# Three transfers and a copy re-timed at the head of a two-layer transformer kernel: the fourth group of x, Wk of the third group, tile 3

## The chip, the cores and the metric

The kernel runs on one core of a Trainium2 chip. The metric is device time in microseconds (us) of one execution; four executions of the kernel before took 1230.28 to 1231.41, median 1230.93. A core has a matrix engine (PE, with its weight loads PEld), VectorE (DVE), ScalarE (ACT), GpSimd (POOL) and SyncE (SP). Here SP issues nearly all loads from memory and the transposing DMAs, and POOL issues the DMAs that move attention data within the core.

## The reference

Input x has 2048 tokens of 1024 features. Two layers follow one another, with the same weights in both; each is attention and then a feed-forward part, both on a layer norm and both added to x. Cut to what matters:

```python
def _A_ref(x, wqkv, wo):                   # 32 heads of 32, window of 8 tokens, 2 apart
    q, k, v = split(x @ wqkv)              # wqkv is 1024 x 3072
    idx = pos[:, None] - 2 * arange(8)     # this token and 7 before it; masked where negative
    attn = softmax(where(mask, q . k[idx] * 32 ** -0.5, -1e9))
    return (attn . v[idx]) @ wo
def _B_ref(x, w1, b1, w2, b2):
    return gelu(x @ w1 + b1) @ w2 + b2     # 1024 -> 3584 -> 1024

for _ in range(2):
    x = x + _A_ref(layernorm(x), wqkv, wo)
    x = x + _B_ref(layernorm(x), w1, b1, w2, b2)
```

Data are bf16; sums in PE's accumulators are f32.

## The kernel before, in words

The 2048 tokens are cut into NG = 4 groups of T = 512, each of four tiles of 128 tokens. A group in a layer is a step n = 0 to 7 (n = 0 to 3 are groups 0 to 3 in layer one). x stays on the core in 16 tiles `x[0]` to `x[15]`; `load_x(g)` issues the four loads (256 KB each) of group g, and `load_x(3)` is the fourth group, `x[12]` to `x[15]`.

A step has these parts, each a Python generator that yields after each chunk of PE work:

- `gen_qkv(n)`: queries, keys and values of the group, eight chunks each. A chunk is eight matmuls (k = 0 to 7) into one accumulator bank `acc`, which ACT casts into `qT`, `kT` or `vT`.
- `gen_wo(n)`: the attention output `oT` times wo. For each tile and half of the features, eight matmuls run over c = 0 to 7, and DVE adds the result to x.
- `gen_ffn1(n)` and `gen_ffn2(n)`: the feed-forward part.

Between them is the attention proper. DVE multiplies queries and keys (`new_prod`, `add_prods`), POOL's DMAs gather the products by head (`gather`, into `abc` in the first steps), DVE and ACT form the softmax (`logits`, `weights`, giving `a`), POOL's DMAs spread its weights over the partitions (`spread`: four DMAs `abc<-a` of 256 KB), and `av(n, c)` on DVE multiplies them with the values and writes `oT[:, c]`. A list of side calls in `stage` says after which chunk of PE work such a call is emitted.

The layer norm gives normalized tiles `xn`, and `xnT`, their transpose, is what PE reads. Mostly a transposing DMA from SP makes it. At the head, PE transposes tiles 2 and 3 of group 0 itself (`transpose_on_pe`), between the rows of the first queries (`queries_of_raw`), and ACT copies the accumulator bank into `xnT` (`copy_transposed`, in as many pieces as `parts` names).

Weights come in halves: `load_qkv(which)` issues two loads of 1 MB, h0 for k = 0 to 3 and h1 for k = 4 to 7, of Wq (0), Wk (1) or Wv (2). All weights share `wpool` with five buffers, taken in turn, so a load waits until PE has made its last use of the half loaded five places earlier. In program order the halves at the head are: Wq h0, h1, Wk h0, h1, Wv h0, h1 of group 0, the same six of group 1, the same six of group 2, and then the two halves of wo for `gen_wo(0)`.

Each engine's instructions run in the order in which they stand on it. The Tile framework sets that order from a simulation; where the kernel wants its own, `InOrder` records each instruction, chains them while `on` is true, and `hold()` puts all later ones behind the last. For SP this is on at the head and ends with step 0. What stands there on SP before the change, in order: transposes of group 1 and of tiles 0 and 1 of group 2, `load_x(3)`, Wq h0, h1 and Wk h0 of group 1, the transposes of tiles 2 and 3 of group 2 (`ln_end`; they read `xn` in buffers named `qT`), and Wk h1, Wv h0, Wv h1 of group 1, and then Wq of group 2.

Step 1 is built with `mix=NCH // 2`: four query chunks, then keys and queries in turn, then the remaining keys; its Wv is loaded before the ninth chunk (`i == NCH`). Step 2 has all its queries first. The order on PE at the head is step 0's q, k, v, step 1's q, k, v, then queries, keys and two value chunks of step 2, then `gen_wo(0)`, and then the rest of step 2's values. `between(0, 1)`, after chunk 11 of step 1, holds `logits(0)`, `weights(0)` and `spread(0)`; `av(0, c)` follows from chunk 12 on, and `load_b1` issues four small POOL DMAs in step 2. The statistics of group 3's layer norm (`ln_stats_ahead(3)`, on ACT) are the first reader of `x[12]` to `x[15]`.

Of the kernel before, what the change touches and what calls it, by code (L numbers as in the profile page):

```python
# [17 lines left out]
def kernel(  # L18
# [19 lines left out]
    _, S, D = A_x.shape  # L38
# [12 lines left out]
    KD = D // P  # L51
    KF = F // P
    NCH = D // P
    HP = P // H
# [7 lines left out]
    wqkv_v = A_wqkv.rearrange("(k p) f -> p k f", p=P)  # L62
# [15 lines left out]
    def acc_tile():  # L78
        return psum.tile([P, T], F32, name="acc", bufs=8)
# [23 lines left out]
    vec, act, pool, sp = InOrder(nc.vector), InOrder(nc.scalar), InOrder(nc.gpsimd), InOrder(nc.sync)  # L103
# [6 lines left out]
    def pe(inst):  # L110
        if last_pe[0] is not None:
            dep_order(inst, last_pe[0], "PE program order")
        last_pe[0] = inst
        return inst

    def mm(*args, **kwargs):
        return pe(nc.tensor.matmul(*args, **kwargs))  # L117
# [3 lines left out]
    def load_x(g, t0=0, t1=NTT, engine=None):  # L121
        for tt in range(t0, t1):
            t = g * NTT + tt
            (engine or sp).dma_start(x[t][:], x_in[t * P:(t + 1) * P, :])

    def load_qkv(which, between=None):
        tiles = []
        for h in range(2):
            wt = wpool.tile([P, KD // 2, D], BF16, name="wt")
            sp.dma_start(wt[:], wqkv_v[:, h * (KD // 2):(h + 1) * (KD // 2), which * D:(which + 1) * D])  # L130
            if h == 0 and between:
                between()
            tiles.append(wt)
        return tiles
# [88 lines left out]
    def transpose_on_pe(xn, out, bank, parts=(0, KD)):  # L223
        pst = bank[:].bitcast(BF16).rearrange("p (k t) -> p k t", t=P)
        for k in range(KD):
            pe(nc.tensor.transpose(pst[:, k, :], xn[:, k * P:(k + 1) * P], ident[:]))  # L226
        copy_transposed(out, bank, parts)

    def copy_transposed(out, bank, parts):
        pst = bank[:].bitcast(BF16).rearrange("p (k t) -> p k t", t=P)  # L230
        for k0, k1 in zip(parts[:-1], parts[1:]):
            act.copy(out[:, k0:k1, :], pst[:, k0:k1, :])
# [8 lines left out]
    first_early, first_late = [], []  # L241
# [67 lines left out]
    def queries_of_raw(wq, qT):  # L309
        raw, spread_stats, rest = st.pop("raw")  # L310
        first = {}

        def row(c, k):
            if k == 0:
                first[c] = acc_tile()
            mm(first[c][:, 0:NT + 2], lhsT=wq[k // (KD // 2)][:, k % (KD // 2), c::NCH], rhs=raw[:, k, :],
               start=(k == 0), stop=(k == KD - 1), skip_group_check=True)

        part = attp.tile([P, NCH, NT], F32, name="abc")

        def finish(c):
            vec.scalar_tensor_tensor(out=part[:, c, :], in0=less, scalar=first[c][:, NT:NT + 1], in1=first[c][:, 0:NT],
                                     op0=ALU.mult, op1=ALU.add)
            pool.tensor_tensor(out=qT[:, c, 0:NT], in0=part[:, c, :], in1=rstd, op=ALU.mult)

        for k in range(KD):
            for c in range(7):
                row(c, k)
                if (k, c) == (0, 6):
                    bank = acc_tile()  # L330
                if (k, c) == (2, 6):
                    less, rstd = spread_stats(bank)
                    rest()
                if (k, c) in ((5, 3), (7, 6)):
                    transpose_on_pe(*first_late.pop(0), bank)
        act.on = False
        act.hold()
        for c in range(7):
            finish(c)
        for k in range(KD):  # L340
            row(7, k)
        vec.on = False
        return lambda: finish(7)
# [13 lines left out]
    def qkv_chunk(wts, c, xnT, ps=None, k0=0, k1=KD, t0=0, t1=NTT):  # L357
        if ps is None:
            ps = acc_tile()
        for k in range(k0, k1):  # L360
            mm(ps[:, t0 * P:t1 * P], lhsT=wts[k // (KD // 2)][:, k % (KD // 2), c::NCH], rhs=xnT[:, t0:t1, k, :],
               start=(k == 0), stop=(k == KD - 1), skip_group_check=t1 - t0 < NTT)
        return ps
# [21 lines left out]
    def gen_qkv(n, defer=False, qk_pool=None, v_late=False, qk_next=None, v_first=False, mix=0):  # L385
        g = n % NG
        xnT = xa.pop(n)
        s = st[n]
        s["prods"] = []
        qk_pool = qk_pool or attp  # L390
        if v_first:
            wv = load_qkv(2)
        wq = wq_first if n == 0 else load_qkv(0)
        if n > 0 and not v_first:
            wk = load_qkv(1)

        def values():
            vT = attp.tile([P, NCH, HALO + T], BF16, name="vT", bufs=2)
            s["vT"] = vT
            act.on = n > 2  # L400
            if g == 0:
                pool.memset(vT[:, :, 0:HALO], 0.0)
            else:
                (act.copy if n > 1 else pool.tensor_copy)(vT[:, :, 0:HALO], st[n - 1]["vT"][:, :, T:T + HALO])
            act.on = False
            for c in range(NCH):
                ps = qkv_chunk(wv, c, xnT)
                act.copy(vT[:, c, HALO:], ps[:])
                yield

        if v_first:
            yield from values()
            wk = load_qkv(1)
        qT = qk_pool.tile([P, NCH, T], BF16, name="qT")
        if n == 0:
            last = queries_of_raw(wq, qT)
            for xn, out in first_early:
                sp.dma_start_transpose(out, xn.rearrange("s (k p) -> s k p", p=P))
            wk = load_qkv(1, lambda: load_x(1, 2, 3))
            load_x(1, 3, 4)  # L420
            load_x(2)
            early_tiles = ln_early((1, None), (2, qk_next))
            for tt in range(2):
                next(early_tiles)
                if tt == 0:
                    last()
            wv = load_qkv(2)
            for _ in early_tiles:
                pass
            vec.hold()  # L430
            load_x(3)
            sp.on = False
            sp.hold()
        kT = qk_pool.tile([P, NCH, HALO + T], BF16, name="kT")
        s["qT"], s["kT"] = qT, kT
        act.on = n > 2
        if g == 0:
            pool.memset(kT[:, :, 0:HALO], 0.0)
        else:
            (act.copy if n > 1 else pool.tensor_copy)(kT[:, :, 0:HALO], st[n - 1]["kT"][:, :, T:T + HALO] if n < 3 else khalo[:])  # L440
        act.on = False

        def query(c):
            t0 = 2 if n == 0 else 0
            ps = qkv_chunk(wq, c, xnT, t0=t0)
            act.copy(qT[:, c, t0 * P:], ps[:, t0 * P:])

        def key(c):
            ps = qkv_chunk(wk, c, xnT)
            act.copy(kT[:, c, HALO:], ps[:])  # L450
            if not defer:
                new_prod(n, c)

        ahead = mix or NCH
        turns = [(query, c) for c in range(ahead)]
        for c in range(NCH):
            turns.append((key, c))
            if ahead + c < NCH:
                turns.append((query, ahead + c))
        for i, (chunk, c) in enumerate(turns):  # L460
            if i == NCH and n > 0 and not v_late and not v_first:
                wv = load_qkv(2)
            chunk(c)
            yield
        if g + 1 < NG and n > 1:
            act.copy(khalo[:], kT[:, :, T:T + HALO])
        if not v_first:
            if v_late:
                wv = load_qkv(2)
            yield from values()  # L470
# [49 lines left out]
    def between(n, m):  # L520

        vec.on = True
        for c in range(2):
            new_prod(m, c, False)
        add_prods(m, 0)
        logits(n)
        add_prods(m, 1)
        weights(n)
        spread(n)
        new_prod(m, 2, False)  # L530
        add_prods(m)
        vec.on = False

    def spread(n):

        s = st[n]
        a = s.pop("a")
        abc = attp.tile([P, NTT, W, P], BF16, name="abc")
        s["abc"] = abc
        s["oT"] = attp.tile([P, NCH, T], BF16, name="qT" if n == N - 1 else "oT")  # L540
        for j in range(HP):
            pool.dma_start(abc[j::HP, :, :, :], a[:])

    def av(n, c):
        s = st[n]
# [183 lines left out]
    n = N - 2  # L729
# [35 lines left out]
```

## Time and profile before

| | us |
|---|---|
| median of four runs | 1230.93 (1230.28 to 1231.41) |
| profiled execution, whole | 1230.72 |
| its span | 1228.9 |
| PE busy | 1220.3 (99%) |
| DVE busy | 865.8 (70%) |
| ACT busy | 315.0 (26%) |
| POOL busy | 121.8 (10%) |
| TensorE clock granted | 1.0 throughout |
| DMA: 227.18 MB, mean | 185 GB/s |
| in the first 59 us | 304 GB/s, DMA share 1.03 |

A row of a timeline gives the start, the length, the engine and line, the operation, output<-input by the program's names, the number of instructions merged, and in brackets the idle time of the engine before it and what ended that. L92 and L117 are helpers through which nearly all instructions go, so one reads by tiles. SPq is SP's queue: its lengths are those of issues, and when the data land is told by the trace's landing records. Times are counted from the start of the span.

### The profile page before, as it was taken

What the parts mean: (1) busy time and instruction counts of PE and PEld (TensorE: products, weight loads), DVE (VectorE), ACT (ScalarE), POOL (GpSimd) and SP (SyncE); (2) the same over time, 40 slices, a digit from 0 to 9 for tenths busy, and PEclk for the clock granted to TensorE, in tenths of its full rate; (3) what the DMA queues carried; (4) which work ended last, traced back from release to release, by engine and by line L of the source; (5) the groups of instructions that cost most, each with busy time, mean ns of one, the idle gap of its engine ahead of it and who ended that gap; (6) DMA issues with size and microseconds to landing.
All of it is one profiled execution on the core that took longest, in us unless ns stands there. A gap on an engine that the chain in (4) does not pass through costs nothing.

```text
span 1228.9 us, 13973 instructions
## 1 busy us (share of the span) xinstructions
PE 1220.3 (99%) x5719; PEld 632.1 (51%) x5769; DVE 865.8 (70%) x926; ACT 315.0 (26%) x497; POOL 121.8 (10%) x217
## 2 busy tenths in 40 slices
PE   9999999999999999999999999999999999999998
PEld 7666544456444564446544465444654444444444
DVE  8989898998898999375993759937598797011001
ACT  5343253014410234202441024410244001300310
POOL 2430006010101101100001000000000002000000
PEclk9999999999999999999999999999999999999999
DMA  9974665766637645856547565576664558446441
GB/s 317 291 206 157 184 201 182 201 175 203 217 130 245 186 150 166 237 172 176 159 158 232 171 171 180 157 216 201 171 202 144 188 194 211 147 160 194 157 136 51
DMA packets 225824, 227.18 MB, mean 185 GB/s; under 512 B 74000, under 2 KB 192928, under 8 KB 223712
## 3 DMA queue, kind: packets, MB, share of 16 engines
q1 hardware_dynamic: 216304, 208.17, 55.5%
q0 software_dynamic: 8880, 17.07, 4.2%
q8 instruction: 45, 0.74, 0.2%
q10 hardware_dynamic: 576, 1.05, 0.2%
q14 instruction: 19, 0.16, 0.0%
HBM read 189.01 MB, written 4.19 MB: 157 GB/s over the span
## 4 chain that ended last, share of the span: by engine, by line
PE 98%; DMA 1%; DVE 0%; issue 0%; ACT 0%
PE acc L117 98%; DMA wt<-in_A_wqkv_dram 0%; DMA x<-in_A_x_dram 0%; DVE stats L92 0%; PE acc L226 0%; ACT xnT L92 0%; ACT vT L92 0%; PE acc L289 0%; DVE mvs L92 0%; DVE x L92 0%; ACT stds L92 0%
## 5 line engine op out<-in xcount | busy, mean ns | idle before, releaser
L117 PE MATMUL acc<-xnT,wt 128*128 128x512 bf16 (+1 forms) x3328 | 713.2, 377 | 1.5 <-DMA wt<-in_A_wqkv_dram 1.3
L117 PEld LDWEIGHTS <-wt 128*128 128x128 bf16 x3392 | 400.6, 119 | 320.7 <-DMA wt<-in_A_wqkv_dram 1.9
L117 PE MATMUL acc<-wt,hT 128*128 128x512 bf16 (+1 forms) x1780 | 386.0, 376 | 2.1
L117 PEld LDWEIGHTS <-hT 128*128 128x128 bf16 x1820 | 178.1, 98 | 209.0
L92 DVE TENSOR_TENSOR big<-big 128x2048 bf16<-128x2048 bf16 (+2 forms) x185 | 245.1, 1353 | 2.2
L92 ACT ACTIVATE hT<-acc,b1T 128x512 bf16<-128x512 f32 x224 | 151.8, 689 | 323.2 <-PE acc L117 323.1
L92 DVE TENSOR_TENSOR big<-qT,kT 128x4096 bf16<-128x4096 bf16 x64 | 143.9, 2285 | 37.5 <-ACT kT L92 35.8
L92 DVE TENSOR_TENSOR big<-abc,vT 128x4096 bf16<-128x4096 bf16 x64 | 144.7, 2285 | 14.2 <-DMA abc<-a 10.2
L92 DVE TENSOR_TENSOR tmp<-acc,b2bc 128x512 f32<-128x512 f32 x56 | 38.6, 690 | 153.7 <-PE acc L117 150.5
L92 ACT CAST qT<-acc 128x512 bf16<-128x512 f32 (+1 forms) x64 | 35.5, 559 | 276.6 <-PE acc L117 276.6
L117 PE MATMUL acc<-wt,oT 128*128 128x512 bf16 x440 | 97.4, 379 | 0.4
L92 DVE BATCH_NORM_STATS2 stats<-x 128x6 f32<-128x512 bf16 x116 | 77.5, 682 | 4.7 <-DMA x<-in_A_x_dram 3.6
L117 PEld LDWEIGHTS <-oT 128*128 128x128 bf16 x448 | 43.7, 98 | 52.9 <-DVE oT L92 0.4
L92 DVE TENSOR_TENSOR x<-acc,big 128x512 bf16<-128x512 f32 (+1 forms) x9 | 5.7, 633 | 90.0 <-PE acc L117 90.0
L92 POOL TENSOR_TENSOR rstd<-mv,eps_t 128x1 f32<-128x1 f32 x48 | 14.7, 306 | 502.0 <-DVE mv L92 502.0
L92 ACT CAST vT<-acc 128x512 bf16<-128x512 f32 x64 | 37.5, 586 | 101.8 <-PE acc L117 101.8
L92 ACT CAST kT<-acc 128x512 bf16<-128x512 f32 x64 | 37.2, 584 | 61.8 <-PE acc L117 61.7
L92 DVE TENSOR_TENSOR x<-acc,x 128x512 bf16<-128x512 f32 x64 | 42.9, 671 | 4.1 <-PE acc L117 3.7
L92 DVE TENSOR_SCALAR xn<-x,mv,rstd 128x1024 bf16<-128x1024 bf16 x48 | 26.2, 546 | 20.1 <-POOL rstd L92 19.9
L92 DVE TENSOR_TENSOR x<-tmp,x 128x512 bf16<-128x512 f32 x56 | 38.6, 690 | 1.4
L92 POOL DMA_DIRECT2D big<-big x24 | 13.3, 565 | 212.2 <-DVE big L92 212.2
L92 ACT ACT_TABLE_LOAD x17 | 21.8, 1283 | 43.6 <-DVE e L92 30.5
(82 smaller groups left out, 304.1 us busy)
## 6 DMA issues: line engine op xcount, KB each, us to landing
wt<-in_B_w_dram SPq DMA_DIRECT2D x56, 1024.0 KB, 5.6
wt<-in_B_w_dram SPq DMA_DIRECT2D x64, 896.0 KB, 4.9
wt<-in_A_wqkv_dram SPq DMA_DIRECT2D x46, 1024.0 KB, 5.6
wt<-in_A_wo_dram SPq DMA_DIRECT2D x16, 1024.0 KB, 5.0
abc<-a POOLq DMA_DIRECT2D x32, 256.0 KB, 5.2
big<-big POOLq DMA_DIRECT2D x24, 256.0 KB, 3.9
out_dram<-x SPq DMA_DIRECT2D x31, 128.0 KB, 1.8
x<-in_A_x_dram SPq DMA_DIRECT2D x14, 256.0 KB, 5.4
```

The costliest lines, as they stand in the source:

```text
L92: inst = f(*args, **kwargs)
L117: return pe(nc.tensor.matmul(*args, **kwargs))
```

## The change

Three edits:

1. `load_x(3)` is taken out of step 0, where it stood behind the early transposes, and is issued in step 1 behind the loads of its Wv (`n == 1`, before the ninth chunk). On SP the four loads now stand between Wv h1 of group 1 and Wq h0 of group 2.
2. `load_qkv` gets an argument `behind`: its first half waits on a semaphore for the completion of an earlier DMA. Step 2 gives it the last of the four spread DMAs of group 0 for Wk, so Wk h0 of group 2 is issued when `spread(0)` has landed.
3. In `queries_of_raw` ACT's copy of the transposed tile 3, at `(k, c) == (7, 6)`, is made in two pieces of four k each; that of tile 2 stays whole.

PE, DVE and POOL have the same instructions in the same order as before. ACT has one copy more. On SP only the four x loads change their place, and one load waits in addition.

```diff
-    def load_qkv(which, between=None):
+    def load_qkv(which, between=None, behind=None):
...
-            sp.dma_start(wt[:], wqkv_v[:, h * (KD // 2):(h + 1) * (KD // 2), which * D:(which + 1) * D])
+            load = sp.dma_start(wt[:], wqkv_v[:, h * (KD // 2):(h + 1) * (KD // 2), which * D:(which + 1) * D])
+            if h == 0 and behind:
+                tc.add_manual_dep(load.ins, behind.ins.name,
+                                  mybir.DependencyInfo(mybir.DependencyClass.Sync, mybir.DependencyReason.DATA),
+                                  reason="behind the spread of the weights")
...
-                if (k, c) in ((5, 3), (7, 6)):
+                if (k, c) == (5, 3):
                     transpose_on_pe(*first_late.pop(0), bank)
+                if (k, c) == (7, 6):
+                    transpose_on_pe(*first_late.pop(0), bank, (0, KD // 2, KD))
...
-            wk = load_qkv(1)
+            wk = load_qkv(1, behind=last_spread[0] if n == 2 else None)
...
             vec.hold()
-            load_x(3)
             sp.on = False
             sp.hold()
...
                 wv = load_qkv(2)
+                if n == 1:
+                    sp.hold()
+                    load_x(3)
...
+    last_spread = [None]
+
     def spread(n):
...
-            pool.dma_start(abc[j::HP, :, :, :], a[:])
+            last_spread[0] = pool.dma_start(abc[j::HP, :, :, :], a[:])
```

## The prediction

> **What bounds the kernel now.** I read the page's chain of work first. PE holds 98% of it at full granted clock, so only a stretch in which PE stands still can be won. The chain in order of time names the places. Its columns are start, length (us), what.
>
> ```profile
> 14.22 1.02 ACT xnT L92
> 15.25 0.04 issue
> 15.29 37.95 PE acc L117 x207
> 53.24 5.84 DMA wt<-in_A_wqkv_dram
> 59.09 0.04 issue
> 59.13 65.19 PE acc L117 x301
> ```
>
> Twice PE waits for something the diff touches: at 15.29 for ACT's copy of the transposed tile 3, at 59.13 for a weight half. From 59.13 to the last store the chain is PE alone. PE's list of waits has two more, both in the first 8 us, which the diff leaves alone:
>
> ```profile
> PE acc L117 <- DMA wt<-in_A_wqkv_dram: 1.3, 1, 1.3
> PE acc L117 <- DVE vT L92: 1.0, 1, 1.0
> PE acc L117 <- ACT vT L92: 0.3, 1, 0.3
> PE acc L117 <- ACT xnT L92: 0.2, 1, 0.2
> ```
>
> Idle time understates the loss, since a 512-column matmul is booked with 379 ns while successors start 216 ns apart (ACT's casts of eight-matmul chunks come every 1.73 us). PE's timeline gives the starts:
>
> ```profile
> 56.80 1.03 PE L117 MATMUL acc<-xnT,wt 128*128 128x512 bf16 x4
> 59.13 1.73 PE L117 MATMUL acc<-xnT,wt 128*128 128x512 bf16 x7 [1.30 <-DMA wt<-in_A_wqkv_dram]
> 14.48 0.61 PE L117 MATMUL acc<-vT,wt 128*128 128x258 bf16 x4
> 15.29 0.38 PE L117 MATMUL acc<-xnT,wt 128*128 128x256 bf16 x2 [0.20 <-ACT xnT L92]
> ```
>
> The fourth matmul before 59.13 started at 57.83 - 0.38 = 57.45, its successor was due at 57.67 and came at 59.13: 1.46 us, with 0.06 in the next step (273 ns instead of 216): **1.52 us**. At 15.29: last start 15.09 - 0.27 = 14.82, due at 14.93 (258 columns step by 0.11): **0.36 us**. Together 1.88 us, 0.15% of the time: this is the ceiling.
>
> Which weight? On SP's queue the last line is Wk of group 1, second half (h1), issued at 53.24, behind two transposes whose issue takes 3.8 and 3.3 us, behind x of group 3 and three other halves:
>
> ```profile
> 37.45 2.00 SPq L92 DMA_DIRECT2D x<-in_A_x_dram  x4
> 39.55 1.58 SPq L92 DMA_DIRECT2D wt<-in_A_wqkv_dram  x3
> 45.98 3.82 SPq L92 DMA_TRANSPOSE xnT<-qT  x1
> 49.89 3.26 SPq L92 DMA_TRANSPOSE xnT<-qT  x1
> 53.24 0.53 SPq L92 DMA_DIRECT2D wt<-in_A_wqkv_dram  x1
> ```
>
> One more place has no wait but no room either. At 123.94 PE begins `gen_wo(0)`; its eighth matmul (c = 7) is due 7 x 0.216 us later, at 125.45. DVE's timeline:
>
> ```profile
> 91.06 4.50 DVE L92 TENSOR_TENSOR big<-abc,vT 128x4096 bf16<-128x4096 bf16 x2 [4.78 <-DMA abc<-a]
> 124.60 0.76 DVE L92 TENSOR_TENSOR oT<-big 128x512 bf16<-128x512 bf16 x2
> ```
>
> The last oT is written at 125.36, 0.09 us before that. DVE ran from 29.55 to 86.29 without a gap, so an earlier PE does not move it; it then stood 4.78 us for the spread weights.
>
> **What the Trainium skill says.** "DMA: Bandwidth & Descriptors", Issuing engines are not separate DMA queues: transfers of SP and POOL run on the same 16 engines and interleave. The trace agrees: the four spread DMAs of group 0, issued from 82.05 while two 1 MB halves issued by SP at 78.38 and 79.24 moved (DMA share 1.09 in 78 to 92), landed in 5.2 to 7.3 us each, those of group 1 at 186.05 in 2.3 to 3.2. "Perfetto Trace Analysis", DMA Instruction — HWDGE (DVE, Sync): an issue's recorded length includes waiting for the descriptor generator, not the movement. The trace has transposes issued in 1.23 us at 130.84 and in 3.82 behind loads. Same page, Optimizing Scalar/DVE Operations: a ScalarE instruction on PSUM carries about 51 ns of overhead; that prices the added copy.
>
> **Tile 3's copy in halves.** One ACT copy of 1.01 us (128x1024) becomes two of 512. Nearest rows: the PSUM copy of 768 takes 0.78, casts of 512 take 0.59 alone and 0.52 apart in a row. First half 14.22 + 0.57 = 14.79, before 14.93. Second half 14.22 + 1.02 + 0.05 (the page's overhead) = 15.29; rows k = 0 to 3 take 4 x 0.11, so it is wanted at 15.36. Gain 0.36; bounds 0.2 (second half 0.15 late) and 0.36. ACT's next work, the qT cast at 16.36, has 1.1 us of room.
>
> **x of group 3 moved.** Four DMAs of 256 KB leave SP's queue at 37.45 and come after Wv h1 of group 1.
>
> - Ahead. Wq h0, h1 and Wk h0 of group 1 start at 37.45 instead of 39.55 (their buffers were free). Their landings were 46.93, 50.64, 53.32. One MB of x less is 2.7 us at the queue's own pace (Wk h0 landed 2.68 after Wq h1), so Wk h0 lands at 49.8 to 50.6. In all four crowded transposes (26.45, 30.46, 45.98, 49.89) the issue ended 0.2 to 0.8 us before the landing of the load two places ahead. So the two transposes, still started by DVE at 45.98, end near 47.2 and 50.3, and Wk h1, whose buffer (Wv h0 of group 0) PE frees near 49, goes at 50 to 50.7 and lands 5.1 (alone, at 71.47) to 5.84 later: 55.1 to 56.5. It is due at 57.67 - 0.36 = 57.31. The **1.52 us** go, with 0.8 to 2.2 to spare; at worst 0.
> - Behind. Wv h1 waits for PE at 71.47, now 69.6. The four issues (2.0 us) and 1 MB (2.7 us) fall between it and Wq h0 of group 2, issued at 72 and landing near 80; its first chunk starts near 90.8 (first qT cast 94.78 before). Wq h1, at 76.5, lands at 82.6 instead of 83.48. The lanes that x waits on are those of loads long landed. x itself is first read by `ln_stats_ahead(3)` on ACT past 120. Cost 0.
>
> **Wk of group 2 behind the spread.** SP now stops at Wk h0 of group 2 (79.24 before) until the last spread DMA lands. Queued behind it is Wk h1, which waits for PE's last Wv matmuls anyway (92.19, now 90.3), and everything after that. Keys of group 2 start near 106.3 (first kT cast 108.60), now 104.4; a landing 5.1 to 7.4 us after an issue at 87 to 92 is in time by at least 5 us. Cost 0. In return the spread meets at most the end of Wq h1: as at 186.05, where the last landed 4.82 us after the first issue, it lands at 82.05 + 4.8 = 86.9, at most 89 with a backlog, against 90.98. `av` starts at 86.9 to 89 instead of 91.06 and the last oT comes at 121.2 to 123.3. With PE 1.88 ahead it is wanted at 123.57. No gain by itself, but it **keeps** the other two: without it PE would stand 125.36 - 123.57 = 1.79 us here, and 0.09 of the 1.88 would be left.
>
> **What is late next.** Wo h1 lands at 124.72 and its first matmul is due at 124.80. It waits for a buffer PE frees, so it moves along with PE; 0 to 0.2 us may be lost. After that every load waits for PE's releases too, and shifts with it.
>
> **Sum.** -1.52 - 0.36 + 0.05 (Wo, or a late half) = -1.83. The profiled execution took 1230.72 (span 1228.9 and 1.8 around it), so 1228.9; the median of the four runs is 0.2 above that execution: **1229.1 us**. A measurement of this kernel can tell about 0.2% (2.46 us) from no change, so this most likely counts as none.
>
> **Rivals.**
>
> 1. *The spread stays late* (0.12). At 383.65 spread DMAs took 8 to 11 us beside loads, so crowding can return: x puts 1 MB more in front of Wq h1. A landing up to 89.3 (1.79 before 91.06) costs nothing; after that each us is lost on PE. Landing at 90 to 91 gives 1229.8 to 1230.8. Against it: by my count the queue is empty at 82.6.
> 2. *The stall stays* (0.10). The transposes hold SP as long as before for a reason of their own, and Wk h1 still lands near 59; the x move then does not do what it says. Only the copy pays: 1230.6; half the stall left gives 1229.9. For it: they are long in every crowded place. Against: 1.26 us at 34.76 once loads had landed.
> 3. *Slower* (0.05). The same crowding beyond break-even: from a landing at 91 on PE's wait in `gen_wo(0)` exceeds the gain, and from 93.5 the kernel is 0.2% slower (1233.4). That takes some 4 MB in front of the spread; I count under 0.5.
> 4. *More than the ceiling* (0.05): a step I take as rigid loosens, 1228.3 or less.
>
> The likeliest (0.68) has its own range, 1228.5 to 1229.6, from the bounds above and 0.4 us of scatter among runs; a median at its lower end crosses 0.2%. That lower end and case 4 make faster 0.18; slower is case 3 and something unseen, 0.07; the rest is the same. Low 1228.2; high 1231.1 takes in cases 1 and 2.
>
> **What would show it.** Right: no PE wait at 57 to 58 for `wt`; the `xnT` wait gone at 15; Wk h1 issued near 50.5; the two transposes issued in under 3 us each; `abc<-a` landing before 89; DVE's gap before `av` under 3 us; `gen_wo(0)` on PE at 122.1. Wrong: a PE or PEld wait for oT near 123, for `wt` near 57 or 104, or a `DMA abc<-a` gap of 4 us or more on DVE.

## The result, and the profile after

The changed kernel takes **1229.06 us** (median of 39 runs, 1228.75 to 1229.42) against 1231.1 (59 runs, 1229.86 to 1233.05). The ratio is 0.9983, 95% interval [0.9978, 0.9987]: 0.17% faster, and an unchanged time (1.0) lies outside the interval. The gain is under the 0.2% that the prediction took as the least that can be told from no change, and the median is 0.04 us from the forecast of 1229.1. The runs also lie closer together: standard deviation 0.15 us against 0.64.

PE's list of waits in the profile after (engine, line and what it waited for; us in total, times, longest):

```profile
PE acc L117 <- DVE vT L92: 1.0, 1, 1.0
PE acc L117 <- ACT vT L92: 0.3, 1, 0.3
```

Both waits that the diff touches are gone; the two left lie in the first 8 us. ACT's copy of tile 3 now comes in two pieces, 1.07 us together where one piece took 1.01, and PE's timeline runs through where it stood before:

```profile
14.51 1.07 ACT L92 COPY xnT<-acc 128x512 bf16<-128x512 bf16 x2 [0.69 <-PE acc L230]
```

```profile
15.21 45.13 PE L117 MATMUL acc<-xnT,wt 128*128 128x256 bf16 x240
...
122.34 14.01 PE L117 MATMUL acc<-wt,oT 128*128 128x512 bf16 x62
```

I call row 7 the eight matmuls of the last chunk (c = 7) of group 0's first queries, which PE makes while ACT copies tile 3. From row 7's first matmul (14.02 before, 14.31 after) to `gen_wo(0)` (123.94 and 122.34) PE needs 108.04 instead of 109.91 us, from the unrounded times 1.88 less. SP's queue shows how:

```profile
37.86 1.66 SPq L92 DMA_DIRECT2D wt<-in_A_wqkv_dram  x3
46.14 3.16 SPq L92 DMA_TRANSPOSE xnT<-qT  x2
49.39 1.09 SPq L92 DMA_DIRECT2D wt<-in_A_wqkv_dram  x2
```

The three halves start where x started; the two transposes take 3.2 us together instead of 7.1, and Wk h1 goes at 49.39 instead of 53.24. It lands at 55.44, some 2 us before PE wants it. And DVE:

```profile
88.34 4.50 DVE L92 TENSOR_TENSOR big<-abc,vT 128x4096 bf16<-128x4096 bf16 x2 [1.89 <-DMA abc<-a]
...
121.88 0.75 DVE L92 TENSOR_TENSOR oT<-big 128x512 bf16<-128x512 bf16 x2
```

The gap before `av` is 1.89 instead of 4.78 us, and the last oT comes at 122.63. PE wants it at 122.34 + 1.51 = 123.85, so 1.2 us are to spare where there were 0.09.

### The profile page after: what moved, and what is told of

Its sections match the earlier page's. It is cut to its first block, busy times and chain, and to the rows that moved or that the text cites. A ratio compares the mean times of both kernels' runs of the same rounds, so it can differ in the third digit from the quotient of the medians.

```text
span 1227.4 us, 13975 instructions
## 1 busy us (share of the span) xinstructions
PE 1220.2 (99%) x5719; PEld 632.4 (52%) x5769; DVE 865.7 (71%) x926; ACT 314.9 (26%) x498; POOL 121.8 (10%) x217
## 4 chain that ended last, share of the span: by engine, by line
PE 99%; DMA 0%; DVE 0%; issue 0%; ACT 0%
PE acc L117 99%; DMA x<-in_A_x_dram 0%; DVE stats L92 0%; PE acc L230 0%; ACT vT L92 0%; PE acc L293 0%; DVE mvs L92 0%; DVE x L92 0%; ACT stds L92 0%
```

## The experiments

The median of the kernel before differs by up to 0.4 us from one occasion to another: it is 1231.1 beside the result, 1231.39 beside e1 to e4, 1231.02 beside e5 and e6. Differences of that size between the medians of two versions are therefore read together with the traces.

The account on which most verdicts rest: from the trace I take the start-to-start distances of PE's matmuls, and book as loss what exceeds the regular step (0.216 us, or 0.108 in the short ones). Subtracted from the time between row 7's first matmul and the end of the span, this should leave the same number everywhere. The column "oT, wo" is the loss at the start of `gen_wo(0)`: in e1 and e7 a wait for oT, in the profile after, e2 and e5 one for wo's second half, which landed just before the matmul that uses it (after: 123.20 and 123.25).

| profile | tile 3 | Wq h1 | Wk h1 | oT, wo | sum | row 7 to end | less sum |
|---|---|---|---|---|---|---|---|
| before | 0.36 | 0 | 1.52 | 0 | 1.88 | 1214.90 | 1213.02 |
| before (e8) | 0.36 | 0 | 0.78 | 0 | 1.14 | 1214.16 | 1213.02 |
| before (e9) | 0.36 | 0.66 | 1.41 | 0 | 2.43 | 1215.45 | 1213.02 |
| before (e10) | 0.36 | 0.32 | 1.53 | 0 | 2.21 | 1215.23 | 1213.02 |
| before (e11) | 0.36 | 0.54 | 1.43 | 0 | 2.33 | 1215.36 | 1213.03 |
| after | 0 | 0 | 0 | 0.04 | 0.04 | 1213.05 | 1213.01 |
| after (e12) | 0 | 0 | 0 | 0 | 0 | 1213.04 | 1213.04 |
| e1 no wait | 0 | 0 | 0 | 0.52 | 0.52 | 1213.55 | 1213.03 |
| e7 no wait | 0 | 0 | 0 | 0.55 | 0.55 | 1213.59 | 1213.04 |
| e2 whole copy | 0.36 | 0 | 0 | 0.14 | 0.50 | 1213.51 | 1213.01 |
| e3 x early | 0 | 0.44 | 1.48 | 0 | 1.92 | 1214.96 | 1213.04 |
| e4 transposes later | 0 | 0 | 0 | 0 | 0 | 1213.02 | 1213.02 |
| e5 wait alone | 0.36 | 0 | 0.74 | 0.12 | 1.22 | 1214.23 | 1213.01 |

The last column agrees within 0.03 us, so from row 7 on all that these kernels gain or lose is in these four places.

**e1, the wait of Wk taken out.**

```diff
-            wk = load_qkv(1, behind=last_spread[0] if n == 2 else None)
+            wk = load_qkv(1)
```

> The changed kernel with Wk of group 2 no longer waiting for the spread (x moved and the copy halved stay). Theory (the wait keeps the gain of the other two): PE has no wait at 15 and at 57, arrives at gen_wo(0) about 1.88 us before the kernel before, and stands there for oT, since Wk h0 crowds the spread again: the last spread DMA lands at 90 to 91, DVE idles 3.5 to 5 us before av, PE waits 1.0 to 1.9 us for oT in gen_wo(0); 1230.0 to 1231.0 us. Rival (the wait is a by-stander; the spread is quick enough without it): the spread lands by 89, no PE wait for oT, 1229.1 us.

Measured: 1229.67 us (21 runs, 1229.32 to 1230.68), ratio to the kernel before 0.9987 [0.9981, 0.9994]. PE's timeline has the wait for oT, and DVE's the longer gap:

```profile
123.93 6.34 PE L117 MATMUL acc<-wt,oT 128*128 128x512 bf16 x28 [0.24 <-DVE oT L92]
```

```profile
89.92 4.49 DVE L92 TENSOR_TENSOR big<-abc,vT 128x4096 bf16<-128x4096 bf16 x2 [3.58 <-DMA abc<-a]
```

The mechanism is the theory's, the size is not: the last spread DMA landed at 89.84 and PE lost 0.52 us, half the least that was expected. The median, 0.6 us above the changed kernel's, says about the same. Three of the 21 runs took 1230.15 to 1230.68, up to 1.6 us more than the changed kernel; none of these has a profile, so what they lost is open.

**e7, the same kernel for a second profile.**

> e1 once more, for one more profile. It asks how far the landing of the spread scatters. If e1's 89.84 is typical, the last spread DMA lands within 0.5 us of it and PE loses 0.3 to 1.0 us for oT; if the 90.98 of the kernel before is as likely here, PE loses 1.5 us or more.

Measured: 89.79, and 0.55 us lost; 1229.48 us in one run. e1's profile is typical of the quicker runs; the three slower ones above remain without one.

**e2, tile 3's copy in one piece.**

```diff
-                    transpose_on_pe(*first_late.pop(0), bank, (0, KD // 2, KD))
+                    transpose_on_pe(*first_late.pop(0), bank)
```

> The changed kernel with tile 3's copy in one piece. Theory: PE's wait of 0.2 us for xnT near 15 is back and moves everything after it by 0.36 us; no other wait; from PE's first queries matmul on xnT to gen_wo(0) the distance is that of the changed kernel, from the end of row 7 to it 0.36 us more; 1229.4 us. Rival (the second half of the copy was late and cost what the first gained): the same distance as in the changed kernel within 0.1 us, 1229.1 us.

Measured: 1229.44 us (21 runs, 1229.11 to 1229.64). PE's timeline:

```profile
15.42 107.29 PE L117 MATMUL acc<-xnT,wt 128*128 128x256 bf16 x528 [0.19 <-ACT xnT L92]
```

From row 7 to the first matmul on `xnT` it is 1.26 us (14.16 to 15.42) against 0.90 with the halves (14.31 to 15.21): 0.36 us, as expected. From there to `gen_wo(0)` it is 107.13 us in both, so the second half of the copy was not late. The median is 0.38 above, of which a part may be the occasion and the 0.14 us for wo.

**e3, x back in its old place** (`load_x(3)` in step 0 again, not in step 1).

> The changed kernel with x of group 3 back in its old place (the Wk wait and the halved copy stay). Theory (the landing of Wk h1 of group 1 is set by SP's queue, not by PE): the stall before key chunk 0 is back and swallows the 0.36 us of the copy too: Wk h1 issued near 53.3, landing near 59.1, PE idle 1.6 us in the records; DVE's gap before av is short and does not help; 1230.9 us, as before. Rival (the parts add up): the stall is back at 1.3 us idle and the copy's gain is kept, 1230.6 us. Second rival: x is not what holds Wk h1, no stall, 1229.1 us.

Measured: 1231.11 us (13 runs, 1229.56 to 1232.2), ratio 0.9997 [0.9989, 1.0006]: no faster than before, though two of the three edits are in. PE's timeline:

```profile
51.15 7.13 PE L117 MATMUL acc<-xnT,wt 128*128 128x512 bf16 x32 [0.22 <-DMA wt<-in_A_wqkv_dram]
59.54 64.97 PE L117 MATMUL acc<-xnT,wt 128*128 128x512 bf16 x300 [1.26 <-DMA wt<-in_A_wqkv_dram]
```

The 0.36 us of the copy are swallowed, as the theory had it, but in two bites: part at Wq h1 (landing 51.11), which I had not counted as a place, the rest at Wk h1.

**e4, x early, but the two transposes behind Wk h1.**

```diff
+            if n == 1:
+                for t in end_transposes:
+                    dep_order(t, last_wk[0], "transposes behind Wk")
...
```

`end_transposes` are the two of `ln_end`, `last_wk` is the load of Wk h1; the other lines record the two and put x back.

> As e3 (x in its old place), but the two transposes of group 2's tiles 2 and 3 stand behind Wk h1 of group 1 on SP instead of ahead of it. Theory (x made Wk h1 late only by way of the transposes, whose issue holds SP until the loads ahead have landed): Wk h1 is issued near 49.5, as soon as PE frees its buffer, lands by 56.5, no PE wait near 57, 1229.1 us with the 1 MB of x still ahead of it. Rival (the bytes of x in the queue themselves make it late): Wk h1 lands at 58.5 or later and PE waits 1 us or more, 1230.5 us or more.

Measured: 1229.41 us (21 runs, 1228.77 to 1230.65), ratio 0.9983 [0.9977, 0.999], no loss on PE at all in the profile (1229.26 us). SP's timeline, in which the four weight halves end with Wk h1 (issued at 49.28 by itself):

```profile
37.66 2.00 SPq L92 DMA_DIRECT2D x<-in_A_x_dram  x4
39.76 9.89 SPq L92 DMA_DIRECT2D wt<-in_A_wqkv_dram  x4
49.74 7.31 SPq L92 DMA_TRANSPOSE xnT<-qT  x2
```

With x's 1 MB still ahead, taking the transposes out of Wk h1's way is enough in this execution, and in the median. So SP's standing in the transposes is what made Wk h1 late. The bytes are not free either: it landed at 57.23, outside the expected 56.5, against 55.44 with x moved. That is about 0.5 us before PE wants it, and the runs lie further apart than the changed kernel's (standard deviation 0.50 against 0.15 us, the longest 1230.65); that Wk h1 comes too late in the longer ones is likely and not shown.

**e5, the wait of Wk alone.**

> The kernel before with one edit alone: Wk of group 2 waits for the spread of group 0. Theory: DVE's gap before av falls from 4.8 us to 1 to 2.5 us and the last oT comes 2 to 4 us earlier, but PE still has its two waits (0.2 us for xnT, 1.3 us for wt) and arrives at gen_wo(0) when it did; 1230.9 to 1231.2 us, no change. Rival (the spread was already on PE's path): 0.3 us or more faster, under 1230.7 us.

Measured: 1231.18 us (13 runs, 1230.2 to 1232.74), ratio 1.0004 [0.9996, 1.0012]. DVE's gap fell to 2.08 us:

```profile
89.37 2.29 DVE L92 TENSOR_TENSOR big<-abc,vT 128x4096 bf16<-128x4096 bf16 x1 [2.08 <-DMA abc<-a]
```

The last oT came at 123.67, 1.7 us earlier (2 to 4 had been expected), and PE did not profit: no gain by itself.

**e6, 1 MB more ahead of the spread** (the changed kernel without the wait; x right behind Wk h0 of group 2).

```diff
-            wk = load_qkv(1, behind=last_spread[0] if n == 2 else None)
+            wk = load_qkv(1, (lambda: (sp.hold(), load_x(3))) if n == 2 else None)
...
-                if n == 1:
-                    sp.hold()
-                    load_x(3)
```

> The changed kernel without the Wk wait and with x of group 3 placed right behind Wk h0 of group 2 on SP, so that 1 MB more stands in the queue when the spread of group 0 is issued at 82. Theory (loads queued ahead delay the spread by 2.7 us per MB, and PE loses one for one after a landing of 89.4): the last spread DMA lands at 92 to 92.5 instead of 89.8 in e1, PE waits 2.6 to 3.1 us for oT in gen_wo(0), 1231.8 to 1232.2 us, slower than the kernel before. Rival (POOL's DMAs share the engines evenly with SP's and pass the queued loads): landing by 90.5, PE loses 1.2 us or less, 1230.4 us or less.

Measured: 1233.1 us (17 runs, 1231.46 to 1233.77), ratio 1.0013 [1.0006, 1.0021]. The last spread DMA landed at 92.31 and PE lost 2.99 us for oT, both as the theory had it. But the median is 0.9 us above its range. PE's timeline, and then the windows after the wait (start and end, length, PE busy, granted clock, DMA share, GB/s):

```profile
126.41 5.87 PE L117 MATMUL acc<-wt,oT 128*128 128x512 bf16 x18 [2.71 <-DVE oT L92]
```

```profile
122.00:126.40 4.40, 1.65 (x7) 1.00 0.75 257
126.40:127.90 1.50, 1.49 (x7) 0.95 0.00 0
128.00:131.00 3.00, 3.00 (x9) 0.50 0.00 0
132.00:135.00 3.00, 3.00 (x16) 1.00 0.09 17
```

After a pause of 2.9 us, and 1.35 us after PE had started again, the clock fell to half for 3.4 us, from 127.8 to 131.2, and matmuls stepped by 427 ns: another 1.69 us. With both taken off, e6's distance from row 7 to the end, 1217.71, leaves 1213.03, as in the table. Of the 17 runs seven had a mean granted clock of 1.0 and took 1231.5 to 1232.2, close to the expected range; the ten at 0.999 took 1232.9 to 1233.8.

**e8 to e11, the kernel before four times more, and e12, the changed kernel again.**

> The kernel before once more, for one more profile of its spread. If the pause of 2.2 us between the second and the third spread DMA (87.97 to 90.22) belongs to this kernel, it is there again and the last lands near 91; if it is scatter, the four land 0.7 us apart from 87.3 on and the last at 89.4 to 89.8, leaving DVE's last oT 1.2 us earlier than in the first profile.

> The kernel before once more (third profile). Its two profiles so far took 1230.7 and 1230.2 us, below the median of its timed runs (1231.0 to 1231.4), and show PE losing 1.5 and 0.8 us for Wk h1 and 0.4 us for tile 3. Theory: the slower executions lose more at these two places or at oT in gen_wo(0): the loss for Wk h1 lies between 0.7 and 1.6 us and now and then PE waits for oT, so that time minus these losses is the same in every profile within 0.2 us. Rival: some of the scatter lies elsewhere, in waits that the change does not touch, and the rest differs by 0.5 us or more.

> As e9, a fourth profile of the kernel before. Theory: loss for Wk h1 0.7 to 1.6 us; span minus PE's losses the same within 0.2 us. Rival: it differs by 0.5 us or more.

> As e9, a fifth profile of the kernel before. Theory: loss for Wk h1 0.7 to 1.6 us; span minus PE's losses the same within 0.2 us. Rival: it differs by 0.5 us or more.

> The changed kernel once more. Theory: no PE wait at 15, at 57 or for oT again; spread landed by 89; 1228.8 to 1229.4 us. Rival: now and then it has a stall of its own, as the kernel before has.

Measured: 1230.22, 1231.62, 1231.3 and 1231.21 us, and 1228.9. The last spread DMA landed at 89.73, 91.91, 91.55 and 91.47, and at 88.10 in e12: e8 by itself spoke for scatter, the other three have the pause again. The table's last column answers e9's question from row 7 on: there nothing of the scatter lies in a wait that the change leaves alone. By the measure that e9 names, the span minus the losses, the theory misses: it is 1227.0 to 1227.4 in the five profiles, not the same within 0.2 us. The difference lies ahead of row 7, whose first matmul starts between 14.02 and 14.38, in a stretch that the change does not touch. PE did not wait for oT in any of the five. And the theory's two places were three; e9's PE timeline:

```profile
51.72 7.13 PE L117 MATMUL acc<-xnT,wt 128*128 128x512 bf16 x32 [0.44 <-DMA wt<-in_A_wqkv_dram]
60.04 2.16 PE L117 MATMUL acc<-xnT,wt 128*128 128x512 bf16 x9 [1.19 <-DMA wt<-in_A_wqkv_dram]
```

In three of five profiles PE waited for Wq h1 too. The five losses average 2.00 us (9.99 / 5), the two after 0.02; the medians differ by 2.04.

## Why the prediction was right, step by step

- *The ceiling, 1.88 us.* The sum is what the first profile had, and what came (1.88 from row 7 to `gen_wo(0)`). As a ceiling it was wrong: 1.88 was one draw between 1.14 and 2.43. The step that failed is the list of places. It quotes the landing of Wq h1 (50.64) and never sets it against PE's use of that half, which came 0.1 us later; x early makes it late too. Moving x brought that landing to 45.97, and so the change removes this loss as well.
- *Tile 3, 0.36 us.* Shown by e2: 0.36. The 0.05 us booked for the added copy was about right: the two pieces took 1.07 us together, the one 1.01.
- *x moved, 1.52 us.* The path was right: transposes ended at 47.38 and 49.30 (47.2 and 50.3 forecast), Wk h1 issued at 49.39 (50 to 50.7), landing 55.44 (55.1 to 56.5). e3 and e4 show that x acts by way of the transposes. The size is 0.74 to 1.53 us in the seven profiles with x early and the transposes ahead, not a fixed 1.52.
- *Behind: no cost.* Wq h0 and h1 of group 2 landed at 80.48 and 83.15 (80 and 82.6), and PE did not wait. x's four issues stood on SP from 70.29 to 72.44 without a wait.
- *The wait of Wk.* No cost and no gain by itself, as forecast (e5). The spread landed at 88.27, between the 86.9 and the 89 given. Mis-sized is the price of leaving it out: 1.79 us, by keeping the landing of the first profile, 90.98, in which one step between two spread DMAs took 2.26 us. e1 and e7 have no such step, land at 89.8 and lose 0.52 and 0.55. So in the profiles, and by the medians, the wait is worth about half a microsecond, not nearly the whole gain; in single runs it may be worth more.
- *Wo, 0.05 us:* 0.04 and 0 after, 0.14 in e2, 0.12 in e5.
- *The rivals.* The spread staying late in the changed kernel is refuted: it landed at 88.27, and at 88.10 in e12. The stall staying is refuted too. The slower case did not come, but e6, which places x elsewhere, shows its path, and it bites earlier than I put it: with a landing of 92.31 the median is 2.1 us above the kernel before's on the same occasion (1233.1 against 1231.02), since in most runs the clock falls besides; I had put 0.2% at 93.5 and left the clock out. The 4 MB that I thought it takes were too many: 1 MB more than in e1 made the landing 2.5 us later, so by this estimate 93.5 needs about 2 MB more than the changed kernel has. A gain beyond the ceiling came only against the average of the kernel before, 2.04 against 1.88 us; no run was as short as 1228.3.

The scatter had been left out of the reasoning. One profile of a kernel whose loads land within tenths of a microsecond of their use gives one draw. That the median came within 0.04 us of the forecast is in part luck: the forecast started from a median of four runs, 1230.93, that was 0.17 below the median of 59, and took off 1.83 where 2.04 went, and these two errors cancel.

## What to carry to other kernels

A transposing DMA behind queued loads can hold the queue that issues it, as it held SP here for up to 5.24 us; move bytes that nobody needs yet from ahead of it, and look at what stands behind. Where an engine is sped up, ask which other chain arrives at the meeting point unchanged, and give that chain room at the same time. Take several profiles before pricing a stall of a microsecond: list every load that lands within half a microsecond of its use, not only those with a wait in the one trace.

## What the runs showed of the hardware

- *A transpose's issue can last until what is queued ahead has nearly landed.* Before, the two at 45.98 and 49.89 ended at 49.80 and 53.15, and the loads two places ahead on SP landed at 50.64 and 53.32. In e4 the second transpose's issue took 5.24 us and ended at 57.05, with Wk h1 landing at 57.23. In the profile after, with the load two places ahead landed, the first took 1.24 us. What exactly has to be done by then is open. In the 14 profiles the second of these two ends 0.17 to 0.23 us before that landing, but as steadily 1.07 to 1.17 us before the first transpose lands. And at 8.44 and 19.65 of the kernel before, with 256 KB loads of x ahead, the issue took 1.33 and 1.88 us and ended 2.3 and 3.2 us before the landing two places ahead.
- *POOL's packets largely wait for the loads that SP issued earlier.* The prediction reads the trace as agreeing that the two interleave. They share the engines, but the packets do little interleaving: in e4, with no load under way, the first packet of the spread moves 1.14 us after its issue; in the kernel before it moves at 85.27, 3.2 us after its issue at 82.05, and in between 1.1 MB of SP's loads pass. In e6 it is 4.4 us and 1.5 MB.
- *A short pause can halve PE's clock.* "TensorE: Matmul & The Clock Gate" (What's actually happening) of the Trainium skill gives an idle window of about 3.4 us as what throttles. In e6 a pause of 2.9 us, 2.71 in the records, was enough in the profiled execution; the throttled stretch itself, 3.41 us, agrees with the page's window. The measurement decides: here less than that window sufficed. Ten of the 17 runs, the profiled one among them, show the lower mean clock; the pauses of the others were not seen. Less the 1.69 us of the throttle the ten took 1231.2 to 1232.1 us, about what the seven others took, so by this estimate a pause of about the same length throttles one execution and not another. Why is open. The pauses of up to 1.5 us in the kernel before never did it.
- *An instruction fetch comes together with a delay of the spread of 1.3 to 1.9 us.* In all 14 profiles one packet of 16 KB on the instruction queue (q8) starts between 82.9 and 89.2. In the five where it starts within the time over which the four spread DMAs land (before, e3, e9, e10, e11), one step between them is 1.98 to 2.55 us instead of about 0.7. In the nine where it starts earlier, none is over 1.0. There the delay may fall on the first of the four: where the fetch starts 0.9 to 1.5 us after the spread is issued (after, e2, e4, e5, e12), the first lands 4.0 to 4.7 us after its issue, against 2.52 in e3, whose fetch comes later. This coincidence was seen, not tried: no run moved the fetch.
